# The first expert's rows: a trip through DRAM and VectorE in place of TensorE's transposes, with SyncE's DMAs in a written order

## The chip, the cores and the metric

The kernel is one program on one core of a Trainium2 chip. The core's engines run their own instruction streams, each in its own order, and wait for each other through semaphores: TensorE (PE, matrix products and transposes through a product), VectorE (DVE), ScalarE (ACT), GpSimd (POOL) and SyncE (SP), which here does nothing but issue DMAs. POOL issues the indirect DMAs (gathers and scatters by a list of row numbers). The metric is the device time of one execution in microseconds; the kernel before takes 783.3 us (median of three runs, 783.01 to 784.11).

## The reference

x has 2048 tokens of 448 values. Two branches read it, and a gate mixes them.

```python
# A: linear attention, 16 heads of 28; phi = two softmaxes of a per-head map
phi_q = concat([softmax(pq), softmax(-pq)])         # the same for k
o = (phi_q @ (phi_k^T v)) / (phi_q @ sum(phi_k))
a = o @ wo
# B: 8 experts of 448 -> 1792 -> 448, each token to its best two
logits = x @ w_gate;  topk_idx = argsort(-logits)[:, :2]
for e in range(8):
    out += w[e] * (silu(x @ w1[e]) @ w2[e])         # w is 0 for tokens that did not choose e
g = sigmoid((x * gate_w).sum(-1))
return g * a + (1 - g) * b
```

All of it is float32. The kernel keeps that precision by writing a float32 operand as a rounded high part and a low part, and by adding three products.

## The kernel before, in words

Tokens go in 16 tiles of 128. A first loop makes keys, values, queries and the router's logits, tile by tile. A second loop (`for t in range(NT + 2)`, here called the loop over steps t) finishes the attention: step t does `attend(t)` on PE (product `n`), a chain of small operations on VectorE that ends in `w` (`weigh`), a sum on POOL (`om`), and, one and two steps later, the transposes of `om` on PE (`turn(t - 1)`, product `ot`; rounded to `oh`, `ol`) and the projection (`project(t - 2)`, product `ao`), which ScalarE scales into a buffer `aos` (three of them) that SP stores to the output. `n` of a step has one place in PSUM, so PE starts the next step's `n` when `w` is done with it.

Beside this the experts are prepared. Routing ends some steps into the loop: each token has written its number and weight into a table in DRAM (`tabd`), sorted by expert. The experts are taken by rank of size (`byrank`). `table()` reads each expert's part of `tabd` into `tabm` (512 places, 4 chunks of 128) and, for the three largest experts, `tabx` (places beyond 512, at most 40). `rows(lo, hi)` on POOL turns these tables into row numbers (`idm`, `idx`), and `gather` on POOL fetches the rows of the first expert, in 5 chunks c of 128 tokens (the last of 40), as `xg`. The rows must be turned so that the 448 values lie across partitions (`xgh`, `xgl`, high and low parts): `first_tokens(c)` does it for the first expert, `tokens(e, c)` for the others, later.

The variable `k` counts steps from the one in which the last routing store goes out (k = 1 is t = 7 here, k = 2 is t = 8). At k = 2 the first expert's weights of step 0 are loaded (`load(0)`; a step is 256 of the 1792 columns, two DMAs `wr1` and `wr2`), and `load(1)` stands behind the loop. In the last steps of the loop PE already does the first products of expert 0 (`fill_in`, product `hp`). Then the experts follow, with PE as the busy engine to the end: for each pair of weight steps ScalarE rounds the weights (`w1h`, `w2h`), VectorE subtracts (`w1l`, `w2l`), PE does the first layer (`hp`), ScalarE the silu (`hs`), VectorE splits it (`hx`), PE does the second layer (`acc`).

PE, ACT and DVE run in the order in which the code is written (a manual schedule). POOL's instructions in this part keep the written order too (`in_turn`). SP's DMAs are put in order by a scheduler that estimates times, except where `follow` gives an order: `behind_(i)` makes a DMA stand behind the one that was given to it last (`met["sp"]`). Before, only weight loads were given to it, so the scheduler could place `load(1)` among the loop's stores.

The constants that matter: `ROWS = 1` and `ASKED = {1: (0, 1, 2), 2: (3, 4)}`: chunks 0 to 2 are gathered at k = 2, chunks 3 and 4 at k = 3. `nm = 4` is the number of whole chunks, `P = 128`, `EX = 40`.

Of the kernel before, what the change touches and what calls it, by code (L numbers as in the profile page):

```python
# [8 lines left out]
F32 = mybir.dt.float32  # L9
F32R = mybir.dt.float32r  # L10
BF16 = mybir.dt.bfloat16
I32 = mybir.dt.int32
# [6 lines left out]
P = 128  # L19
# [40 lines left out]
STORES = {}  # L60
LASTS = 1
PLAIN = (2, 3)
VAHEAD = 6
AHEAD = 2
WARM = (4, 3)
# [25 lines left out]
def gated_mix(ctx: ExitStack, tc: tile.TileContext, xt, xq, wk, wq, wv, wphi, wo, w12, out):  # L91
# [15 lines left out]
    def bank(tag, name):  # L107
        pool, n = banks[tag]
        return pool.tile([P, 512], F32, tag=tag, name=name, bufs=n)
# [21 lines left out]
    def in_turn(i, kind=None):  # L131
        if runs["on"]:
            if kind is None or kind != runs["kind"]:
                runs.update(before=runs["last"], last=[], kind=kind)
            for o in runs["before"]:
                follow(i, o)
            runs["last"].append(i)
        return i
# [126 lines left out]
    tabm = cst.tile([P, E * nm, 2], F32, name="tabm")  # L265
    tabx = cst.tile([P, LARGE, 2], F32, name="tabx")
    idm = cst.tile([P, E * nm], I32, name="idm")
    idx = cst.tile([EX, LARGE], I32, name="idx")
    idq = cst.tile([P, E, 4 * nm + 2], I32, name="idq")
    nc.gpsimd.memset(idq, 0)  # L270
    byrank = cst.tile([P, E], I32, name="byrank")
# [505 lines left out]

    raws, wts = {}, {}

    def load(s):  # L780
        e, q = divmod(s, F // 256)
        if q == 0:
            for r in range(e, E if e else 1):
                if r not in whose:
                    whose[r] = nc.values_load(byrank[0:1, r:r + 1], engines=SPONLY, min_val=0, max_val=E - 1)
        keep = narrow(e) and q >= KEPT
        raws[s] = stage(pm, whose[e], q, f"_{s}", 5, (pf, "kept", F // 256 - KEPT) if keep else None)


    def halve(s, layer):  # L790
# [6 lines left out]
        yield  # L797
        nc.vector.tensor_tensor(out=l, in0=raws[s][layer - 1], in1=h.bitcast(F32), op=ALU.subtract)  # L798

    xg = {}  # L800
    x_rows = xq.rearrange("(s a) k -> s (a k)", a=4)

    def extra(e):
# [13 lines left out]
    def gather(e, c, behind):  # L817
        t = pm.tile([P, 4, P], F32, tag="xg", name=f"xg{e}{c}", bufs=nm + 1)
        xg[e, c] = t
        ids, m = (idm[:, e * nm + c:e * nm + c + 1], P) if c < nm else (idx[:, e:e + 1], EX)  # L820
        after(in_turn(nc.gpsimd.indirect_dma_start(out=t[0:m].rearrange("p a k -> p (a k)"), out_offset=None, in_=x_rows,
                                                   in_offset=bass.IndirectOffsetOnAxis(ap=ids, axis=0))), behind)

# [30 lines left out]
        nc.vector.tensor_tensor(out=xl[:, 0:n], in0=src[:, 0:n], in1=xh[:, 0:n].bitcast(F32), op=ALU.subtract)  # L854


    def tokens(e, c):
        if c == 0:
            pool = pf if e % 2 else pw
            xg[e] = (pool.tile([P, 4, CAP], F32R, tag="xgh", name=f"xgh{e}", bufs=1),  # L860
                     pool.tile([P, 4, MAIN] if e >= LARGE else [P, 3, CAP], F32R, tag="xgl", name=f"xgl{e}", bufs=1))
        xgh, xgl = xg[e]
        if (e, c) not in xg:
            return
        t = xg[e, c]
        n, m = (4, P) if c < nm else (-(-extra(e) // 32), extra(e))
        xt_ = pm.tile([P, 4, P], F32, tag="xt", name=f"xgt{e}{c}")
        for b in range(n):
            nc.vector.transpose(xt_[:, :, b * 32:(b + 1) * 32], t[:, b].rearrange("p (c k) -> p c k", c=4))
        yield  # L870
        m = min(m, ROOMS[e] - c * P)
        at = slice(c * P, c * P + m)
        both(xgh[:, :, at], xgl[:, :, at], xt_[:, :, 0:m], e >= LARGE)


    def first_tokens(c):
        m = P if c < nm else EX
        t = xg[0, c][0:m]
        x4 = pm.tile([P, 4, 4, 32], F32, tag="xt", name=f"x40{c}")[0:m]
        in_turn(nc.gpsimd.tensor_copy(x4, t.rearrange("p a (c k) -> p c a k", c=4)))  # L880
        yield
        tp = bank("A", f"xgt0{c}")
        v = tp[:, 0:4 * m].rearrange("p (c n) -> p c n", c=4)
        for i in range(4):
            nc.tensor.transpose(v[:, i], x4[:, i].rearrange("p a k -> p (a k)"), ident[0:m, 0:m])
        if c == 0:
            xg[0] = (pw.tile([P, 4, CAP], F32R, tag="xgh", name="xgh0", bufs=1),
                     pw.tile([P, 3, CAP], F32R, tag="xgl", name="xgl0", bufs=1))
        at = slice(c * P, c * P + m)
        both(xg[0][0][:, :, at], xg[0][1][:, :, at], v)  # L890

    pb_stack.close()
    pc_stack = ExitStack()
# [62 lines left out]
    def leave_row(t, o):  # L958
        ao = pc.tile([P, D], F32, tag="ao", name=f"aos{t}", bufs=3)
        nc.scalar.activation(ao, o[:, 0:D], AF.Copy, scale=gt[:, t:t + 1])  # L960
        rows_done.append(nc.sync.dma_start(out[t * P:(t + 1) * P, :], ao))

    def table():
        for r in range(E):
            v = nc.values_load(byrank[0:1, r:r + 1], engines=SPONLY, min_val=0, max_val=E - 1)
            todo = [(tabm[:, r * nm:(r + 1) * nm], tabd[bass.ds(v * OWN, MAIN), :], P)]
            if r < LARGE:
                n = extra(r)
                for h in range(copies(r)):
                    todo.append((tabx[h * n:(h + 1) * n, r:r + 1], tabd[bass.ds(v * OWN + MAIN, n), :], n))  # L970
            for dst, src, p in todo:
                i = nc.sync.dma_start(dst, src.rearrange("(c p) two -> p c two", p=p))
                after(i, sc)

    def rows(lo, hi):
        in_turn(nc.gpsimd.tensor_scalar(idm[:, lo * nm:hi * nm], tabm.bitcast(I32)[:, lo * nm:hi * nm, 0], float(S - 1), None,
                                op0=ALU.min))
        if lo < LARGE:
            hi = min(hi, LARGE)
            in_turn(nc.gpsimd.tensor_scalar(idx[:, lo:hi], tabx.bitcast(I32)[0:EX, lo:hi, 0], float(S - 1), None, op0=ALU.min))  # L980

    def quarters():
        for a in range(4):
# [267 lines left out]
    for t in range(NT + 2):  # L1251
        if t - 1 in QASKS:
            signs(EQ[QASKS[t - 1]], pq[QASKS[t - 1]])
        elif t == 0:
            signs(EQ[6], pq[6])
        if t < RANKS:
            advance(QSTEPS.get(t, 2))
        early = t in EARLY
        for u in TOPS.get(t, ())[:early]:
            top[u] = tops(EQ[u], f"q{u}", pr)  # L1260
        if at is not None and t == at + 1:
            store(LASTS, behind)
            table()
        if t < NT:
            n_ = attend(t)
        behind = [reached["n"]]
        store(STORES.get(t, 3) if at is None or at == NT else 0, behind)
        if at is None and not routes and t >= RANKS:
            routes.append(ranks())
            at = NT  # L1270
        if at == NT and len(stores) <= LASTS and not routes:
            at = t
        k = t - (NT if at is None else at)
        if k == ROWS + 1:
            rows(0, 1)
        for c in ASKED.get(k - ROWS, ()):
            gather(0, c, behind)
        if t < NT:
            weigh(t, n_)
        advance(2 if t >= RANKS else WSTEPS.get(t, 0))  # L1280
        for u in TOPS.get(t, ())[early:]:
            top[u] = tops(EQ[u], f"q{u}", pr)
        if t + QAHEAD in top:
            drop(EQ[t + QAHEAD], top[t + QAHEAD])
        rows_too = t + 2 < NT
        if rows_too:
            flip(t + 2, True)
            if t >= 1:
                turn(t - 1, True)
        if 1 <= t and t + QAHEAD - 1 < NT:  # L1290
            raise_(t + QAHEAD - 1)
        if t >= 2:
            if t == NT + 1:
                fill_in()
            leave_row(t - 2, project(t - 2))
        if t == NT:
            fill_in()
        if 1 <= t <= NT and not rows_too:
            turn(t - 1, False)
        if t in QASKS:  # L1300
            ask(QASKS[t], some=(0 if t else 5, 11))
        if t == NT - 1:
            fill_in()
        if t == PEND:
            pe_stack.close()
            pm = ctx.enter_context(tc.tile_pool(name="pm", bufs=2, side="right", reuse_waits="tile"))
            pw = ctx.enter_context(tc.tile_pool(name="pw", bufs=1, side="right", reuse_waits="tile"))
            ph = ctx.enter_context(tc.tile_pool(name="ph", bufs=2, side="right", reuse_waits="tile"))
        if k == ROWS + 3:
            rows(1, E)  # L1310
        if k == 2:
            load(0)
            splits += [halve(0, 1), halve(0, 2)]
        part_way()
        if ROWS + 2 <= k < ROWS + 3 + nm:
            g = first_tokens(k - ROWS - 2)
            next(g)
            coming.append(g)
        if SPLIT <= t < SPLIT + 3 and splits:
            if next(splits[0], 0) == 0:  # L1320
                del splits[0]
                if splits:
                    next(splits[0])
# [177 lines left out]
```

## Time and profile before

| | us |
|---|---|
| median of three runs | 783.3 |
| the profiled execution | 784.29 |
| its span, first to last instruction | 782.5 |
| of which: PE busy | 772.5 |
| loop over steps t with the first expert's preparation | about 100 to 210 |
| first `hp` of expert 0 | 201.82 |

The profile is one execution of the program. Its page gives the busy time of each engine, a strip of 40 slices of the span, the DMA queues, and the costliest groups of instructions; the trace behind it can be asked for the instructions of an engine in order of time, for who waited for whom, and for busy times in stretches. A row of a timeline gives start and duration in us, engine, line, operation, what is written and read (`hp<-xgh,w1h`: product hp of xgh and w1h), partitions x elements, how many are merged into the row (x4), and, in brackets, how long the engine sat idle before it and what ended that. `SPq` rows are the issues of DMAs; a DMA's data land later. PE and its weight loads (PEld) overlap.

Two rows of the strip show the whole span, 19.6 us a digit: PE is at nine tenths or more in nearly every slice, and its clock is full in all of them.

```profile
PE   9999999999999999999999999999999999999996
PEclk9999999999999999999999999999999999999999
```

### The profile page before, as it was taken

To read this page: it belongs to the slowest core of one execution; us is meant where nothing else is said; L and a number is where in the kernel's file an instruction comes from. 1 tells how busy PE (TensorE), PEld (TensorE's weight loads), DVE (VectorE), ACT (ScalarE), POOL (GpSimd) and SP (SyncE) were. 2 spreads that over 40 slices of the span, in tenths; PEclk is the share of its full clock that TensorE was granted. 3 is DMA by queue.
4 is the path that set the end of the run, shared out by engine and by line. 5 is a ranking of instruction groups with operands and counts; after the bars stand their busy time and mean duration, and the time that the engine had idled before them with its cause. 6 is when DMAs were issued, how large, how long until landed. Compare 5 with 4: busy or idle time off the path is not lost. (4 is left out here: it accounts for less than half of the span.)

```text
span 782.5 us, 18423 instructions
## 1 busy us (share of the span) xinstructions
PE 772.5 (99%) x7548; PEld 721.0 (92%) x7548; DVE 482.0 (62%) x1047; ACT 308.7 (39%) x521; POOL 338.3 (43%) x320
## 2 busy tenths in 40 slices
PE   9999999999999999999999999999999999999996
PEld 7888888888999999998999799999999999999995
DVE  4798978777775865675566345554744555475442
ACT  5543455666523443343333233333433333343220
POOL 5667877885123226413550237054225405523102
PEclk9999999999999999999999999999999999999999
DMA  8420000044343236324633354364345336434502
GB/s 272 132 87 1 2 2 26 28 101 159 100 164 125 73 113 160 127 93 107 167 114 105 69 142 149 113 156 132 123 119 154 131 115 158 136 129 111 172 3 47
DMA packets 39756, 86.37 MB, mean 110 GB/s; under 512 B 11338, under 2 KB 20722, under 8 KB 39668
## 3 DMA queue, kind: packets, MB, share of 16 engines
q1 hardware_dynamic: 29332, 67.88, 26.1%
q0 software_dynamic: 10192, 17.03, 11.2%
q8 instruction: 61, 1.00, 0.6%
q10 hardware_dynamic: 144, 0.23, 0.1%
q14 instruction: 27, 0.22, 0.1%
HBM read 72.31 MB, written 12.82 MB: 109 GB/s over the span
## 5 line engine op out<-in xcount | busy, mean ns | idle before, releaser
L1127 PE MATMUL acc<-w2h,hx 64*128 64x448 f32 (+3 forms) x1088 | 192.3, 363 | 0.1
L1076 ACT ACTIVATE hs<-hp 128x272 f32<-128x272 f32 (+4 forms) x154 | 70.8, 483 | 305.9 <-issue 192.5
L829 POOL DMA_INDIRECT xg<-in_xq_dram,idq x114 | 126.6, 1111 | 149.5 <-PE hp L1043 52.2
L1082 DVE CAST hx<-hs 128x504 fp32r<-128x504 f32 (+5 forms) x154 | 55.0, 357 | 203.2 <-ACT hs L1076 203.1
L1127 PEld LDWEIGHTS acc<-w2h,hx 64*128 64x128 f32 (+3 forms) x1088 | 160.4, 182 | 4.5 <-ACT y L1216 1.6
L1127 PE MATMUL acc<-w2l,hx 64*128 64x448 f32 (+3 forms) x544 | 154.3, 363 | 0.0
L1043 PE MATMUL hp<-xgh,w1h 64*128 64x504 f32 (+2 forms) x490 | 146.0, 385 | 0.0
L1043 PE MATMUL hp<-xgh,w1l 64*128 64x504 f32 (+2 forms) x490 | 145.9, 385 | 0.0
L1043 PE MATMUL hp<-xgl,w1h 64*128 64x504 f32 (+2 forms) x490 | 145.8, 384 | 0.0
L995 POOL DMA_INDIRECT out_dram<-y,tabm x30 | 49.3, 1643 | 158.1 <-DVE y L1218 150.8
L1161 PE MATMUL acc<-w2h,hx 128*128 128x448 f32 (+2 forms) x362 | 110.6, 365 | 0.0
L1127 PEld LDWEIGHTS acc<-w2l,hx 64*128 64x128 f32 (+3 forms) x544 | 96.4, 182 | 1.2
L1043 PEld LDWEIGHTS hp<-xgh,w1h 64*128 64x128 f32 x490 | 87.4, 184 | 2.2 <-issue 0.3
L1043 PEld LDWEIGHTS hp<-xgl,w1h 64*128 64x128 f32 x490 | 87.5, 185 | 1.8
L1043 PEld LDWEIGHTS hp<-xgh,w1l 64*128 64x128 f32 x490 | 87.5, 185 | 1.7
L1085 DVE TENSOR_TENSOR hx<-hs,hx 128x276 fp32r<-128x276 f32 (+5 forms) x168 | 84.8, 512 | 5.3
L145 PE MATMUL hp<-xgh,w1h 128*128 128x272 f32 (+1 forms) x336 | 87.9, 289 | 0.0
L145 PE MATMUL hp<-xgh,w1l 128*128 128x272 f32 (+1 forms) x336 | 87.8, 289 | 0.0
L798 DVE TENSOR_TENSOR w1l<-wr,w1h 128x1024 fp32r<-128x1024 f32 x56 | 68.2, 1218 | 11.1 <-ACT w1h L796 9.9
L1161 PEld LDWEIGHTS acc<-w2h,hx 128*128 128x128 f32 (+2 forms) x362 | 67.4, 186 | 6.1 <-issue 0.7
L1161 PE MATMUL acc<-w2l,hx 128*128 128x448 f32 (+2 forms) x188 | 68.7, 365 | 0.0
L145 PEld LDWEIGHTS hp<-xgh,w1h 128*128 128x128 f32 x336 | 63.2, 188 | 0.7
(249 smaller groups left out, 1402.8 us busy)
## 6 DMA issues: line engine op xcount, KB each, us to landing
wr<-in_w_dram SPq DMA_DIRECT2D x56, 512.0 KB, 3.6
wr<-in_w_dram SPq DMA_DIRECT2D x46, 448.0 KB, 4.4
kept<-in_w_dram SPq DMA_DIRECT2D x10, 448.0 KB, 4.2
out_dram<-aos SPq DMA_DIRECT2D x16, 224.0 KB, 5.2
xr<-in_xt_dram SPq DMA_DIRECT2D x10, 256.0 KB, 5.0
xg<-in_xq_dram,idq POOLq DMA_INDIRECT x114, 3.4
xr<-in_xt_dram SPq DMA_DIRECT2D x6, 192.0 KB, 4.3
out_dram<-zero SPq DMA_DIRECT2D x5, 224.0 KB, 3.8
```

Of the source, the lines that this page charges most:

```text
L145: reached["pe"] = nc.tensor.matmul(o, a, b, start=i == 0, stop=i == n - 1)
L798: nc.vector.tensor_tensor(out=l, in0=raws[s][layer - 1], in1=h.bitcast(F32), op=ALU.subtract)
L829: i = nc.gpsimd.indirect_dma_start(out=t[:, b], out_offset=None, in_=xq, in_offset=bass.IndirectOffsetOnAxis(ap=idq[:, e, 4 * c + b:4 * c ...
L995: return nc.gpsimd.indirect_dma_start(out=out, out_offset=bass.IndirectOffsetOnAxis(ap=idx_ap, axis=0), in_=y, in_offset=None, compute_op= ...
L1043: meet(("first", i), a, lambda: nc.tensor.matmul(o[i], l, r, start=n == 0, stop=n == len(rounds) - 1), n == 0)
L1076: nc.scalar.activation(hs[:, tsl], hp, AF.Silu)
L1082: nc.vector.tensor_copy(h[:, tsl], hs[:, tsl])
L1085: nc.vector.tensor_tensor(out=h[:, a + o:b + o], in0=hs[:, a:b], in1=h[:, a:b].bitcast(F32), op=ALU.subtract)
L1127: meet((e, c), a, lambda: nc.tensor.matmul(acc[e][c][:l.shape[1], 0:D], l[half[a]], r[half[a]], start=new, stop=ends and c not in of[k + 1 ...
L1161: i = nc.tensor.matmul(acc[e][c][:l.shape[1], 0:D], l, r, start=fc == 0 and k == 0, stop=fc == NFC - 1 and k == len(pr) - 1)
```

## The change

The first expert's rows are no longer turned by PE. POOL's gather is followed by a write of the chunk to DRAM (`rows_out`, `by_row`) and four reads of it back into the same tile (`rows_in`), each of which puts every fourth 128-value quarter of the chunk's rows onto 32 partitions. Then one blockwise transpose on VectorE (`in_blocks`, 32 x 32 blocks) gives the turned rows; the experts that follow use the same function, so that their four transposes a chunk become one instruction. ScalarE rounds the result as before; the two subtractions move from VectorE to POOL (`xsplit(..., nc.gpsimd)`), one step later, and POOL's copies go. The last chunk is gathered with 64 rows, 24 of them row 0, to fill two blocks.

On SP, the loop's stores, the tables and the writes and reads are all given to `behind_`, in the order of the code. `table()` is cut in two: the first expert's table stays at k = 1, the others go to k = 5, and their conversion `rows(1, E)` from k = 4 to k = 7; `load(0)` goes from k = 2 to k = 4.

```diff
+TABLE = 5
+FIRST_LOAD = 4
...
-        for b in range(n):
-            nc.vector.transpose(xt_[:, :, b * 32:(b + 1) * 32], t[:, b].rearrange("p (c k) -> p c k", c=4))
+        in_blocks(xt_, t, n)
...
+    def rows_out(c):
+        m = P if c < nm else 64
+        by_row[c] = dram.tile([m, 4, P], F32, name=f"by_row{c}")
+        behind_(nc.sync.dma_start(by_row[c], xg[0, c][0:m]))
+
+    def rows_in(c):
+        n = 4 if c < nm else 2
+        for a in range(4):
+            behind_(nc.sync.dma_start(xg[0, c][32 * a:32 * a + 32, 0:n],
+                                      by_row[c][:, a].rearrange("(b t) k -> t b k", b=n)))
+
     def first_tokens(c):
-        m = P if c < nm else EX
-        t = xg[0, c][0:m]
-        x4 = pm.tile([P, 4, 4, 32], F32, tag="xt", name=f"x40{c}")[0:m]
-        in_turn(nc.gpsimd.tensor_copy(x4, t.rearrange("p a (c k) -> p c a k", c=4)))
-        yield
-        tp = bank("A", f"xgt0{c}")
-        v = tp[:, 0:4 * m].rearrange("p (c n) -> p c n", c=4)
-        for i in range(4):
-            nc.tensor.transpose(v[:, i], x4[:, i].rearrange("p a k -> p (a k)"), ident[0:m, 0:m])
+        n, m = (4, P) if c < nm else (2, EX)
+        xt_ = pm.tile([P, 4, P], F32, tag="xt", name=f"xgt0{c}")
+        in_blocks(xt_, xg[0, c], n)
+        yield
...
-        both(xg[0][0][:, :, at], xg[0][1][:, :, at], v)
+        xsplit(xg[0][0][:, :, at], xg[0][1][:, :, at], xt_[:, :, 0:m], nc.gpsimd)
...
         rows_done.append(nc.sync.dma_start(out[t * P:(t + 1) * P, :], ao))
+        behind_(rows_done[-1])
...
-            table()
+            table(0, 1)
...
-        if k == ROWS + 3:
+        if k == TABLE:
+            table(1, E)
+        if k == TABLE + 2:
             rows(1, E)
-        if k == 2:
+        if k == FIRST_LOAD:
             load(0)
...
-        if ROWS + 2 <= k < ROWS + 3 + nm:
-            g = first_tokens(k - ROWS - 2)
+        for lag, move in ((1, rows_in), (0, rows_out)):
+            for c in ASKED.get(k - ROWS - lag, ()):
+                move(c)
+        if ROWS + 3 <= k < ROWS + 4 + nm:
+            g = first_tokens(k - ROWS - 3)
```

What this makes of the engines' order is seen in the built programs. First SP in the second half of the loop. The rows are its DMAs, destination and source; `aos5` is the buffer of step 5's store, `xg00` chunk 0 of the first expert, `wr1_0` and `wr2_0` the weights of step 0. Before, from the last table load on:

```order
L972 DMA tabm_143<-tabd_155 128x4x2
L961 DMA out_0_dram<-aos5_2632 128x448
...
L773 DMA wr1_0_2779<-in_w12_dram 128x1024
...
L773 DMA wr2_0_2780<-in_w12_dram 128x896
...
L773 DMA wr1_1_3573<-in_w12_dram 128x1024
...
L773 DMA wr2_1_3574<-in_w12_dram 128x896
L961 DMA out_0_dram<-aos6_2754 128x448
L961 DMA out_0_dram<-aos7_2884 128x448
```

And of the change, from store 7 to the first of the 15 tables of the other experts:

```order
L972 DMA out_0_dram<-aos7_2792 128x448
L891 DMA xg00_2602<-by_row0_2685 32x4x128 x4
L891 DMA xg01_2604<-by_row1_2687 32x4x128 x4
L891 DMA xg02_2606<-by_row2_2689 32x4x128 x4
L886 DMA by_row3_2807<-xg03_2726 128x512
L886 DMA by_row4_2809<-xg04_2728 64x512
L972 DMA out_0_dram<-aos8_2906 128x448
...
L776 DMA wr1_0_2909<-in_w12_dram 128x1024
...
L776 DMA wr2_0_2910<-in_w12_dram 128x896
L891 DMA xg03_2726<-by_row3_2807 32x4x128 x4
L891 DMA xg04_2728<-by_row4_2809 32x2x128 x4
L972 DMA out_0_dram<-aos9_3016 128x448
...
L984 DMA tabm_143<-tabd_156 128x4x2
```

Twenty reads, two of the five writes and the first weights now stand between store 7 and the tables, which stood ahead of store 5. The second weight step (`wr1_1`, `wr2_1`), which followed the first, stands at the end of the loop, behind store 15:

```order
L972 DMA out_0_dram<-aos14_3495 128x448
L972 DMA out_0_dram<-aos15_3553 128x448
...
L776 DMA wr1_1_3569<-in_w12_dram 128x1024
...
L776 DMA wr2_1_3570<-in_w12_dram 128x896
...
L776 DMA wr1_2_3573<-in_w12_dram 128x1024
```

Here `wr1_1` moved from behind `wr2_0` to behind `aos15`, and `wr1_2` with it. Second, POOL in steps 11 to 14; `om11` is the sum of step 11, `idm` of 28 columns and `idx` are the conversion of the other experts' tables. Before:

```order
L976 TENSOR_SCALAR idm_145<-tabm_143 128x28
L980 TENSOR_SCALAR idx_146<-tabx_144 40x2
L880 COPY x401_2999<-xg01_2688 128x512
L931 TENSOR_TENSOR om11_3043<-w11_3041 128x448
...
L880 COPY x402_3105<-xg02_2690 128x512
L931 TENSOR_TENSOR om12_3149<-w12_3147 128x448
```

And of the change:

```order
L942 TENSOR_TENSOR om13_3253<-w13_3251 128x448
L989 TENSOR_SCALAR idm_145<-tabm_143 128x28
L993 TENSOR_SCALAR idx_146<-tabx_144 40x2
L160 TENSOR_TENSOR xgh0_3104<-xgt02_3209,xgh0_3104 64x128
L161 TENSOR_TENSOR xgl0_3105<-xgt02_3209,xgh0_3104 128x3x128
L942 TENSOR_TENSOR om14_3357<-w14_3355 128x448
```

The conversion moved from ahead of `om11` to behind `om13`, and the copies of the chunks gave way to two subtractions each, those of chunk 2 between the conversion and `om14`.

More of the change, by code (lines that the diff above doesn't have):

```diff
@@ L267, in gated_mix @@
     idm = cst.tile([P, E * nm], I32, name="idm")
-    idx = cst.tile([EX, LARGE], I32, name="idx")
+    idx = cst.tile([64, LARGE], I32, name="idx")
+    nc.gpsimd.memset(idx, 0)
     idq = cst.tile([P, E, 4 * nm + 2], I32, name="idq")
@@ L778, in gated_mix, with expert @@
     raws, wts = {}, {}
+    def expert(r):
+        if r not in whose:
+            whose[r] = nc.values_load(byrank[0:1, r:r + 1], engines=SPONLY, min_val=0, max_val=E - 1)
+        return whose[r]
     def load(s):
         e, q = divmod(s, F // 256)
[L782 to L785, printed above, removed]
         keep = narrow(e) and q >= KEPT
-        raws[s] = stage(pm, whose[e], q, f"_{s}", 5, (pf, "kept", F // 256 - KEPT) if keep else None)
+        raws[s] = stage(pm, expert(e), q, f"_{s}", 5, (pf, "kept", F // 256 - KEPT) if keep else None)
     def halve(s, layer):
@@ L798, in halve @@
         nc.vector.tensor_tensor(out=l, in0=raws[s][layer - 1], in1=h.bitcast(F32), op=ALU.subtract)
-    xg = {}
+    xg, by_row = {}, {}
     x_rows = xq.rearrange("(s a) k -> s (a k)", a=4)
@@ L819, in gather @@
         xg[e, c] = t
-        ids, m = (idm[:, e * nm + c:e * nm + c + 1], P) if c < nm else (idx[:, e:e + 1], EX)
+        ids, m = (idm[:, e * nm + c:e * nm + c + 1], P) if c < nm else (idx[:, e:e + 1], 64)
         after(in_turn(nc.gpsimd.indirect_dma_start(out=t[0:m].rearrange("p a k -> p (a k)"), out_offset=None, in_=x_rows,
@@ L854, in both, with in_blocks @@
         nc.vector.tensor_tensor(out=xl[:, 0:n], in0=src[:, 0:n], in1=xh[:, 0:n].bitcast(F32), op=ALU.subtract)
+    def in_blocks(out_, t, n):
+        nc.vector.transpose(out_[:, :, 0:n * 32].rearrange("p c (b k) -> p b c k", b=n),
+                            t[:, 0:n].rearrange("p b (c k) -> p b c k", c=4))
     def tokens(e, c):
@@ L961, in leave_row, with table @@
         rows_done.append(nc.sync.dma_start(out[t * P:(t + 1) * P, :], ao))
-    def table():
-        for r in range(E):
-            v = nc.values_load(byrank[0:1, r:r + 1], engines=SPONLY, min_val=0, max_val=E - 1)
+        behind_(rows_done[-1])
+    def table(lo, hi):
+        for r in range(lo, hi):
+            v = expert(r)
             todo = [(tabm[:, r * nm:(r + 1) * nm], tabd[bass.ds(v * OWN, MAIN), :], P)]
@@ L973, in table @@
                 after(i, sc)
+                behind_(i)
     def rows(lo, hi):
@@ L979, in rows @@
             hi = min(hi, LARGE)
-            in_turn(nc.gpsimd.tensor_scalar(idx[:, lo:hi], tabx.bitcast(I32)[0:EX, lo:hi, 0], float(S - 1), None, op0=ALU.min))
+            in_turn(nc.gpsimd.tensor_scalar(idx[0:EX, lo:hi], tabx.bitcast(I32)[0:EX, lo:hi, 0], float(S - 1), None, op0=ALU.min))
     def quarters():
```

## The prediction

> **What bounds the kernel now.** I read the page's first part, then the list of what TensorE (PE) waited for over the whole span, then the timelines of each engine between 155 and 216 us, the only stretch in which the first expert's rows are prepared.
>
> ```profile
> PE 772.5 (99%) x7548; PEld 721.0 (92%) x7548; DVE 482.0 (62%) x1047; ACT 308.7 (39%) x521; POOL 338.3 (43%) x320
> ...
> PE n L910 <- DVE w L926: 1.4, 2, 1.0
> ```
>
> PE is busy for 772.5 of 782.5 us, and the longest of its waits for another engine's line is 1.4 us in two pieces (the list gives the sum, the count and the longest). So the time moves by what PE no longer executes, and by each new wait of PE, one for one: the experts that follow have no slack in which PE could catch up. I call a step of the loop over token tiles t; `n`, `om`, `ot`, `ao` of step t are its attention, its sum on GpSimd (POOL), its transpose and its output projection.
>
> **What goes from PE.** First the five transposes of the expert's rows, then the two stalls that stand among them.
>
> ```profile
> 177.14 0.60 PE L885 MATMUL xgt<-ident,x 128*128 128x128 f32 x4
> 177.67 1.16 PE L910 MATMUL n<-B,et 64*64 64x60 f32 x64
> ...
> 184.80 0.47 PE L145 MATMUL ao<-WHo,oh 128*128 128x448 f32 x1 [0.23 <-ACT aos L960]
> ...
> 188.72 1.29 PE L910 MATMUL n<-B,et 64*64 64x60 f32 x64 [0.97 <-DVE w L926]
> ...
> 197.66 0.44 PE L885 MATMUL xgt<-ident,x 40*128 40x40 f32 x4
> 198.03 1.16 PE L910 MATMUL n<-B,et 64*64 64x60 f32 x64
> ...
> 201.47 0.60 PE L943 MATMUL ot<-ident,om 128*128 128x128 f32 x4
> ```
>
> A group of four holds PE from 177.14 to 177.67, 0.53 us; four such groups and the small one (197.66 to 198.03, 0.37) make **2.49 us**. The stalls of 0.23 and 0.97, **1.20 us**, come from one store:
>
> ```profile
> 184.11 0.63 ACT L960 ACTIVATE aos<-ao,gt 128x448 f32<-128x448 f32 x1 [2.14 <-DMA out_dram<-aos]
> ```
>
> ScalarE waited 2.14 us for a buffer of `aos`, whose store stood behind four weight loads. Stores 5 to 8 now go ahead of all weights, so this goes. Next in line is VectorE, whose `w` the `n` of the next step waits for. It gives up two subtractions a step and gets one transpose; the trace has four small ones of the same total size:
>
> ```profile
> 178.49 0.29 DVE L853 TENSOR_TENSOR xgh<-xgt,xgh 64x128 fp32r<-64x128 f32 x1
> 178.80 0.56 DVE L854 TENSOR_TENSOR xgl<-xgt,xgh 128x384 fp32r<-128x384 f32 x1
> ...
> 180.63 1.09 DVE L926 TENSOR_TENSOR w<-n,r 128x896 f32<-128x896 f32 x1
> ...
> 182.52 1.16 PE L910 MATMUL n<-B,et 64*64 64x60 f32 x64
> ...
> 253.82 0.88 DVE L869 STREAM_TRANSPOSE xgt<-xg 128x128 f32<-128x128 f32 x4
> 254.62 1.05 DVE L798 TENSOR_TENSOR w2l<-wr,w2h 128x896 fp32r<-128x896 f32 x1
> ```
>
> That is 0.80 us (253.82 to 254.62) against 0.85 given up, so `w` ends as it did, 0.80 ahead of `n` (181.72 against 182.52), and 0.53 less on PE leaves 0.27: nothing is added or won. The same edit in the later experts lies beside a PE that never waits for it: nothing. Alone, these parts would bring `ot` of step 14 from 201.47 to 201.47 - 3.69 = **197.78**.
>
> **What the tables cost.** The other experts' 15 table loads leave their place before the weights and stand behind 20 read-backs of the rows. On POOL the conversion that needs all 15 (`rows(1, E)`) now stands between `om` of 13 and of 14, with two subtractions of chunk 2 behind it; all are ahead of `om` of 14, and `ot` of 14 needs that. Before, the conversion ran at 179.57 without a wait. So I follow SyncE (SP), from the last point that the change leaves alone: store 7 waits for `aos` of 7, whose activation starts at 172.92 and lasts 0.63.
>
> ```profile
> 172.92 0.63 ACT L960 ACTIVATE aos<-ao,gt 128x448 f32<-128x448 f32 x1 [0.27 <-PE ao L145]
> ...
> 175.62 22.75 SPq L961 DMA_DIRECT2D out_dram<-aos  x7
> ...
> 176.09 22.27 SPq L961 DMA_DIRECT2D out_dram<-aos  x6
> ...
> wr<-in_w_dram SPq DMA_DIRECT2D x1, 512.0 KB, 3.6
> wr<-in_w_dram SPq DMA_DIRECT2D x1, 448.0 KB, 5.5
> ...
> 162.01 0.41 SPq L972 DMA_DIRECT2D tabm<-tabd  x1
> ...
> 169.03 3.48 SPq L972 DMA_DIRECT2D tabm<-tabd  x4
> 169.61 2.90 SPq L972 DMA_DIRECT2D tabm<-tabd  x3
> ...
> 172.13 0.37 SPq L972 DMA_DIRECT2D tabm<-tabd  x1
> ...
> DMA to landing us min/median/max: 2.0/3.3/3.8
> ```
>
> Plain issues stand 0.47 apart (175.62 to 176.09). From 173.57, 16 of them (store 7, twelve read-backs, two writes, store 8) end at 181.1. The two loads of weight step 0 follow at 181.1 and 181.7. In the built program SP's DMAs share eight completion counters in turn, so each waits until the one eight before it has landed; the last read-back so waits for the second weight load, 181.7 + 5.5 = 187.2. With store 9 the tables start near **187.8** (186.8 with a landing halfway between the two rows, 189 if each issue ahead takes 0.07 more). Fifteen tables took 162.01 to 172.13 before, 0.72 a step among gathers; undisturbed a step is 0.58 (169.03 to 169.61). I take 0.64 for 14 steps, 9.0 us, and a landing of 2.5 between the last row's 2.0 and 3.8: **199.3**, with ends 186.8 + 8.1 + 2.0 = 196.9 and 189 + 10.1 + 3.8 = 202.9. POOL's share behind that:
>
> ```profile
> 179.57 0.29 POOL L976 TENSOR_SCALAR idm<-tabm 128x28 int32<-128x28 int32 x1
> 179.93 0.21 POOL L980 TENSOR_SCALAR idx<-tabx 40x2 int32<-40x2 int32 x1
> ...
> 63.12 0.46 POOL L158 TENSOR_TENSOR XH<-xr,XH 64x128 fp32r<-64x128 f32 x1
> 63.65 1.01 POOL L159 TENSOR_TENSOR XL<-xr,XH 128x384 fp32r<-128x384 f32 x1
> ...
> 197.97 1.14 POOL L931 TENSOR_TENSOR om<-w 128x448 f32<-128x448 f32 x1 [3.33 <-DVE w L926]
> ```
>
> The conversion takes 0.36 to its second part and 0.21 for that; then 0.53 and 1.01 for the subtractions (rows of the key stage, same shapes) and 1.14 for `om`; with 0.15 of handing over 3.4 us. So `ot` of 14 runs at 199.3 + 3.4 = **202.7**, and PE idles 4.9 us there. VectorE is held too: its transpose of chunk 4 takes the buffer of chunk 2, so it waits for the same subtraction, and `w1l` of the first weights, the attention chain of 15 and `oh`, `ol` of 14 stand behind it.
>
> ```profile
> 199.86 1.22 DVE L798 TENSOR_TENSOR w1l<-wr,w1h 128x1024 fp32r<-128x1024 f32 x1
> ...
> 203.87 0.56 DVE L159 TENSOR_TENSOR ol<-ot,oh 128x384 fp32r<-128x384 f32 x1
> ...
> 204.93 0.78 PE L145 MATMUL ao<-WHo,ol 128*128 128x448 f32 x3
> ```
>
> From `w1l` to the end of `ol` were 4.57 us (199.86 to 204.43). Now the subtraction ends at 201.5, the transpose at 201.9, so `ol` at 206.5; `ao` of 14 wants it 3.46 after `ot` (201.47 to 204.93), at 206.15. With 0.1 for the first `hp`, which waits for `w1l`, that is **0.45** more. Against before PE is then 202.7 - 201.47 + 0.45 = 1.7 us late. This wait also covers the rest: if read-backs landed late and VectorE held PE earlier, up to 4.9 us of it would cost nothing, as would POOL's ten added subtractions. If the tables came early, that cover would be gone.
>
> **What the second weight step costs.** `load(1)` was half of the four loads at 173.31 to 175.5; now it stands behind store 15, which waits for the very last `aos`.
>
> ```profile
> 211.21 0.64 ACT L960 ACTIVATE aos<-ao,gt 128x448 f32<-128x448 f32 x1 [1.84 <-PE ao L145]
> 211.74 1.05 ACT L796 ACTIVATE w1h<-wr 128x1024 fp32r<-128x1024 f32 x1
> ...
> 215.26 0.29 PE L145 MATMUL hp<-xgh,w1h 128*128 128x276 f32 x1
> ...
> 173.31 2.21 SPq L773 DMA_DIRECT2D wr<-in_w_dram  x4
> ```
>
> In the times of before: `aos` of 15 ends at 211.85, its store goes, the load follows 0.6 later (the pitch of the tables) at 212.45, landing between the 3.6 and 5.5 of the two rows above; I take 3.9, near the first, with the store just ahead of it: 216.4. Then `w1h` on ScalarE, 1.05, and `w1l` on VectorE, 1.22: 218.7. PE has work until its `hp` at 215.26 and needs `w1l` from the second matmul on: it waits **3.45 us** (a little less than 218.7 - 215.26 + the hand-overs, since its first matmul needs only `w1h`). The `silu` of the piece before stands behind `w2h` on ScalarE, so the next second layer waits 0.3 more. Nothing hides this; before, the cover was that the load went out 37 us earlier. By the landings it is 3.1 (3.6, and no later wait) to 5.3 in all; I take 3.75.
>
> **The sum.** -2.49 - 1.20 + 4.92 + 0.45 + 3.75 = **+5.4 us**. The profiled execution took 784.29 (span 782.5 and 1.8 around it), so 789.7 for one like it; its median of three is 783.3, 1.0 lower, so 788.7.
>
> **The rivals.**
>
> *The tables land in time* (not slower). The point is 197.78 - 3.4 = 194.4 for the last table. Then PE keeps its 3.69 us and pays only for `load(1)`, 3.1 to 3.75: -0.6 to +0.1, 782.7 to 783.4. For it: POOL and VectorE have room. Against: the low end of the tables is 196.9.
>
> *The queue is slower*: read-backs and tables at the slow ends, 202.9, give 3.6 more, and a `load(1)` at its slow end 1.6: 792.3 to 793.9. For it speaks the 0.72 a step; against, that the gathers which disturbed it are over.
>
> *The clock falls in the long wait.* In this trace it is 1.00 for four microseconds after PE's last matmul, which ends at 775.99, and lower after that:
>
> ```profile
> 778.00:780.00 2.00, 0.00 (x0) 1.00 0.35 97
> 780.00:782.50 2.50, 0.00 (x0) 0.57 0.03 10
> ```
>
> My first wait is 4.9 us, the second 3.5, so the first may reach that point. If PE then ran at 0.57 for as long as it took to fall, 4 us, it would lose 4 x 0.43 = 1.7: 790.4. [...]
>
> *Faster*: both waits are covered by something that I don't see, leaving -3.69: 779.6. Only a load that lands at once would do it, against every landing row above.
>
> **How the numbers follow.** Forecast 62%, slower queue 12%, fallen clock 14%, tables in time 9%, both covered 3%. The range goes from the tables' low end with the cheapest `load(1)` (-3.69 + 2.52 + 0.45 + 3.1 = +2.4, lowered a little towards the rival in time) to the slow queue: 785.0 to 792.5, leaving out the 12% below and a part of the slow queue. A measurement of this kernel tells 0.2%, 1.6 us, from no change; slower by more than that 88%, within it 9%, faster 3%.
>
> **What would show it.** No `xgt` matmuls on PE; PE waiting at `ot` of 14 for `om`, POOL at `idm` (28 columns) for a table; SP's last table issued near 197, `wr` of step 1 after the last store, and PE waiting over 3 us at the third pair of `hp`. If POOL doesn't wait at `idm`, or PE has less than 2 us of waits beside the old ones, the forecast is wrong.

## The result: 794.3 us, slower, and past the end of the range

The changed kernel takes 794.33 us (median of 5 runs, 792.99 to 795.65) against 783.30 before: a ratio of 1.0136, 95% interval 1.0126 to 1.0147. The forecast was 788.7 in a range of 785.0 to 792.5. The direction was right, and the loss is twice the predicted one: 11.0 us instead of 5.4. The profiled execution took 794.56; its span is 792.8, 10.3 longer than before.

First the same lines of the page as before: PE's busy time, and the two strips.

```profile
PE 774.1 (98%) x7528; PEld 721.2 (91%) x7528; DVE 478.4 (60%) x958; ACT 309.1 (39%) x521; POOL 340.9 (43%) x326
...
PE   9999999999689999999999999999999999999997
...
PEclk9999999999899999999999999999999999999999
```

PE has 20 instructions fewer (7528 against 7548) and is nevertheless busy 1.6 us longer. Two slices, the 11th and 12th (198 to 238 us), are no longer full, and in the 11th the clock isn't either. Then the list of what PE waited for, by line: sum, count, longest.

```profile
PE ot L954 <- POOL om L942: 6.3, 1, 6.3
PE hp L147 <- ACT w1h L800: 2.0, 1, 2.0
...
PE hp L147 <- DVE w1l L802: 0.9, 1, 0.9
```

Both predicted waits are there, at the predicted instructions: `ot` of step 14 for `om` 14, and the first `hp` of weight step 1 for its weights. PE's timeline, with the rows that stand against 201.47, 215.26 and the matmul of before with the same place in the program:

```profile
206.02 1.11 PE L954 MATMUL ot<-ident,om 128*128 128x128 f32 x4 [6.31 <-POOL om L942]
...
214.79 0.37 PE L147 MATMUL ao<-WHo,oh 128*128 128x448 f32 x1
...
223.44 0.40 PE L147 MATMUL hp<-xgh,w1h 128*128 128x276 f32 x1 [2.00 <-ACT w1h L800]
224.70 0.39 PE L147 MATMUL hp<-xgh,w1l 128*128 128x276 f32 x1 [0.86 <-DVE w1l L802]
...
231.85 0.29 PE L147 MATMUL hp<-xgh,w1h 128*128 128x276 f32 x1
```

The same points of before's timeline:

```profile
208.77 0.36 PE L145 MATMUL ao<-WHo,oh 128*128 128x448 f32 x1
...
220.89 0.29 PE L145 MATMUL hp<-xgh,w1h 128*128 128x276 f32 x1
```

So PE is 4.55 us late at `ot` 14 (206.02 against 201.47), 6.02 at `ao` 15 (214.79 against 208.77), 8.18 at the first `hp` of weight step 1 and 10.96 at that of step 2 (231.85 against 220.89). That is the whole loss (the spans differ by 10.3), and no wait of PE follows. The prediction had 1.23 (202.7), 1.68, and, with the 3.75 of `load(1)`, 5.43 at the last. Its missing 5.5 us lie in three places: 3.3 before `ot` 14, 1.0 between `ot` 14 and `ao` 15, and 1.2 behind that.

Why `ot` 14 is late is read on SP and POOL. A row's second number is the time from the first issue of a run to the end of its last.

```profile
174.03 0.34 SPq L972 DMA_DIRECT2D out_dram<-aos  x1
174.47 7.06 SPq L891 DMA_DIRECT2D xg<-by_row  x12
181.63 1.00 SPq L886 DMA_DIRECT2D by_row<-xg  x2
...
183.53 0.90 SPq L776 DMA_DIRECT2D wr<-in_w_dram  x2
184.52 6.15 SPq L891 DMA_DIRECT2D xg<-by_row  x8
...
191.93 0.41 SPq L984 DMA_DIRECT2D tabm<-tabd  x1
...
200.99 17.23 SPq L972 DMA_DIRECT2D out_dram<-aos  x6
```

```profile
202.68 0.30 POOL L989 TENSOR_SCALAR idm<-tabm 128x28 int32<-128x28 int32 x1 [10.63 <-DMA tabm<-tabd]
...
204.83 1.13 POOL L942 TENSOR_TENSOR om<-w 128x448 f32<-128x448 f32 x1
```

The order is the predicted one, POOL waits at `idm` for a table, and from `idm` to `ot` it takes 3.34 us (predicted 3.4). But the tables start at 191.93 instead of 187.8. The largest part of that is in the twelve read-backs, which hold SP for 7.16 us (174.47 to 181.63) where 0.47 apart would be 5.64. Taken one by one, eleven of them stand 0.42 to 0.53 apart; the third alone lasts 1.80:

```profile
175.47 1.80 SPq L891 DMA_DIRECT2D xg<-by_row  x1
```

The clock is the other part. Windows of 1 us; the columns behind the width are busy times of PE, PEld, DVE, ACT and POOL with their counts, then the granted clock, the DMA share and GB/s.

```profile
202.00:203.00 1.00, 0.00 (x0) 0.00 (x0) 0.00 (x0) 0.00 (x0) 0.30 (x1) 0.57 0.82 301
203.00:204.00 1.00, 0.00 (x0) 0.00 (x0) 0.00 (x0) 0.63 (x1) 0.78 (x3) 0.50 0.98 369
208.00:209.00 1.00, 1.00 (x6) 1.00 (x6) 0.93 (x3) 1.00 (x1) 0.45 (x1) 0.52 0.06 16
209.00:210.00 1.00, 1.00 (x8) 0.96 (x7) 0.94 (x3) 0.63 (x3) 0.43 (x1) 1.00 0.00 0
...
224.00:225.00 1.00, 0.30 (x2) 0.30 (x3) 0.97 (x4) 0.69 (x2) 0.00 (x0) 1.00 0.95 387
225.00:226.00 1.00, 1.00 (x10) 1.00 (x9) 0.93 (x5) 0.53 (x1) 0.00 (x0) 1.00 0.67 158
226.00:227.00 1.00, 1.00 (x6) 1.00 (x6) 1.00 (x2) 0.82 (x2) 0.00 (x0) 0.52 0.77 188
...
229.00:230.00 1.00, 1.00 (x5) 0.92 (x4) 1.00 (x2) 1.00 (x2) 0.00 (x0) 0.78 0.04 8
```

It falls to half in the first wait (0.57 is 0.14 at full speed and the rest at half, so at 202.14, 2.4 us after PE's last work) and returns at 208.96, three microseconds after PE is at work again. It falls a second time near 226.04, when the second wait is already over, and returns at 229.44.

### The profile page after: what moved, and what is told of

Its sections match the earlier page's. It is cut to its first block, busy times and chain, and to the rows that moved or that the text cites. A ratio compares the mean times of both kernels' runs of the same rounds, so it can differ in the third digit from the quotient of the medians.

```text
span 792.8 us, 18372 instructions
## 1 busy us (share of the span) xinstructions
PE 774.1 (98%) x7528; PEld 721.2 (91%) x7528; DVE 478.4 (60%) x958; ACT 309.1 (39%) x521; POOL 340.9 (43%) x326
## 5 line engine op out<-in xcount | busy, mean ns | idle before, releaser
L147 PE MATMUL hp<-xgh,w1h 128*128 128x272 f32 (+1 forms) x336 | 89.5, 293 | 2.0 <-ACT w1h L800 2.0
L147 PE MATMUL hp<-xgh,w1l 128*128 128x272 f32 (+1 forms) x336 | 89.4, 293 | 0.9 <-DVE w1l L802 0.9
```

What stands on the lines that cost most here:

```text
L147: reached["pe"] = nc.tensor.matmul(o, a, b, start=i == 0, stop=i == n - 1)
```

## The experiments

All ratios are to the kernel before, run on the same chip in the same session: 783.91 us for the first four kernels, 783.37 for the last four, so that times of different sessions compare to about 0.6 us. The first question was whether the two waits are separate and worth what they seem to be.

**Load of weight step 1 earlier.** In the changed kernel:

```diff
         if k == TABLE:
             table(1, E)
+            load(1)
...
-    load(1)
     held = []
```

> The change, with load(1) issued right behind the other experts' tables (step 11) in place of behind store 15. Theory A (two waits made by order, each followed by a fall of the clock): PE's wait at the third pair of hp (3.3 us against before) and the half clock behind it (1.65 us) both go, the wait at ot of 14 stays: 794.3 - 4.9 = 789.4 (788.5 to 790.5). Rival B (the trip through DRAM and its traffic cost the time, the late weights only share it): no more than the shown wait of 2.9 us goes, 791 or above.

Measured: 789.65 us (789.50 to 790.75), ratio 1.0079 (1.0063 to 1.0096), as theory A has it. PE's list has the wait at `ot` (7.4 us) and none at `hp`; the mean clock is 0.995, against 0.991. So `load(1)` behind the loop and what follows from it cost about 4.7 us (794.33 to 789.65, across two sessions; in the traces, from `ot` 14 to the `hp` of weight step 2, it is 4.5), more than the 3.75 of the prediction, which has no clock in it.

**The conversion moved out of the way of `om` 14.**

```diff
-        if k == TABLE + 2:
-            rows(1, E)
...
+    rows(1, E)
     assert not coming and not splits
```

> The change, with the conversion of the other experts' tables, rows(1, E), behind the last subtraction of the first expert's rows on POOL in place of between om of 13 and 14. Theory A: the tables land as late as before (202 to 203) but nobody waits; ot of 14 runs at about 199.6 in place of 206.0, and the clock does not fall there (1.0 to 1.5 us): 794.3 - 6.5 - 1.5 = 786.4 (785.4 to 787.8). Rival B: ot of 14 then waits for something else that the trip made late (read-backs, POOL's subtractions), and the time stays above 789.

Measured: 791.40 us (791.30 to 792.04), ratio 1.0097 (1.0080 to 1.0114): a miss for theory A, and in the range of rival B, though not at B's place. The wait at `ot` 14 is gone, but another stands behind it, at `ao` 14. The rows are of PE, ACT and SP of this kernel:

```profile
204.37 0.47 PE L147 MATMUL ao<-WHo,oh 128*128 128x448 f32 x1 [3.68 <-ACT oh L159]
```

```profile
203.20 0.63 ACT L971 ACTIVATE aos<-ao,gt 128x448 f32<-128x448 f32 x1 [5.72 <-DMA out_dram<-aos]
```

```profile
197.94 2.70 SPq L984 DMA_DIRECT2D tabm<-tabd  x5
200.74 14.21 SPq L972 DMA_DIRECT2D out_dram<-aos  x6
```

`aos` has three buffers. The activation of row tile 13 needs the buffer of store 10, and store 10 stands behind the 15 tables (200.74, the first of the six). On ScalarE `oh` of 14 stands behind that activation, and PE's `ao` of 14 needs `oh`. The same wait is in the changed kernel, under the longer one for `om`:

```profile
203.24 0.63 ACT L971 ACTIVATE aos<-ao,gt 128x448 f32<-128x448 f32 x1 [4.92 <-DMA out_dram<-aos]
```

It ends at 203.24, before `om` 14 is ready, and so costs nothing there.

**Both edits.**

> The two edits together (load(1) behind the tables, rows(1, E) behind the last subtraction). Theory A: both waits and both falls go, 794.3 - 7.9 - 4.9 = 781.5 (780.5 to 783), which is before less the transposes (2.5) and the store's stall (1.2) plus some 2 us for VectorE's wait for read-backs and the like; clock 1.0 until PE ends. Rival B: 784 or above, slower than before, with waits left in the steps 10 to 15.

Measured: 791.99 us (791.02 to 792.22), ratio 1.0101 (1.0085 to 1.0118): a second miss for theory A. Its expectation was written before the third wait was known. No `om` and no `hp` wait is left, and the third has grown to 8.9 us. The two weight loads (201.10) now stand ahead of store 10 as well: it goes out 1.5 us later than in the run before this one, and its buffer comes free 5.6 us behind its issue (207.84 on ScalarE) instead of 2.5.

```profile
209.01 0.74 PE L147 MATMUL ao<-WHo,oh 128*128 128x448 f32 x1 [8.86 <-ACT oh L159]
```

```profile
202.22 18.29 SPq L972 DMA_DIRECT2D out_dram<-aos  x6
```

**Only the stores' order, in the kernel before.** This tests the price of `load(1)` without any of the rest.

```diff
         rows_done.append(nc.sync.dma_start(out[t * P:(t + 1) * P, :], ao))
+        behind_(rows_done[-1])
```

> The kernel before with one line of the change: the loop's stores are given to behind_, so that load(1) goes behind store 15; the transposes on PE and the tables stay as they were. Theory A: PE waits about 3.3 us at the third pair of hp and then loses 1.65 us to the clock if a window falls so; the stall of 1.2 us goes since only two weight loads stand ahead of store 7: 783.3 + 3.3 + 1.65 - 1.2 = 787.0 (785 to 788.5). Rival B (late weights cost little without the trip's traffic): within 1.6 us of 783.3.

Measured: 788.07 us (786.08 to 789.34), ratio 1.0061 (1.0044 to 1.0077). One added line in the kernel before gives the same two waits at `hp`, to a hundredth:

```profile
215.78 0.39 PE L145 MATMUL hp<-xgh,w1h 128*128 128x276 f32 x1 [1.99 <-ACT w1h L796]
217.03 0.39 PE L145 MATMUL hp<-xgh,w1l 128*128 128x276 f32 x1 [0.86 <-DVE w1l L798]
...
222.87 0.29 PE L145 MATMUL hp<-xgh,w1h 128*128 128x276 f32 x1
```

The four runs differ more than most, and with the clock: 786.08, 787.70, 788.44 and 789.34 us at mean granted clocks of 0.999, 0.997, 0.997 and 0.994. Only the run of 786.08 has a trace, and in it the clock stays full; from the other means, the same wait brings a fall in some executions and none in others. Without one it cost 3.4 us, since this edit also takes the 1.2 of the store stall away (783.91 - 1.20 = 782.71). In the traces, from the first `hp` to that of weight step 2, it is 3.61 (200.19 to 222.87, before 201.82 to 220.89).

Then the question was whether three waits, with the clock, are all. A table load that stands behind store 12 instead of store 9 has no store behind it whose buffer is wanted again (16 row tiles, three buffers), and its conversion comes behind `om` 15.

**Tables three steps later, and `load(1)` ahead of them.**

```diff
-TABLE = 5
+TABLE = 8
...
+        if k == 5:
+            load(1)
...
-    load(1)
     held = []
```

> The change with the 15 tables issued three steps later (behind store 12 instead of store 9, so that no store whose buffer is needed again stands behind them; their conversion on POOL moves with them, behind om of 15) and load(1) two steps ahead of them. Theory A (three waits hide each other: om 14 behind the tables' conversion, the store buffers behind the tables, hp behind load(1), and nothing else stands behind them): all three go, PE has no wait over 1 us between 195 and 235 us, the clock stays full, and the time is before's 783.9 on this chip less the 3.7 us of PE's transposes and store stall, plus 0.5 lost early: 780.7 (779.9 to 782.0), faster than before. Theory B (a fourth consumer is behind): a new wait of PE of 2 us or more, 782.5 or more.

Measured: 781.03 us (780.18 to 781.68, 8 runs), ratio 0.9971 (0.9960 to 0.9981): faster than both kernels. No wait of PE between 195 and 235 us is left, and the clock stays full. PE's timeline at the places of the result:

```profile
198.41 0.60 PE L954 MATMUL ot<-ident,om 128*128 128x128 f32 x4
...
212.21 0.29 PE L147 MATMUL hp<-xgh,w1h 128*128 128x276 f32 x1
```

`ot` 14 is 3.06 us ahead of before (198.41 against 201.47) and the `hp` of weight step 1 is 3.05 ahead. That is what the removed transposes and the removed store stall are worth, with what else the change does up to there. POOL still waits 4.9 us for the tables, but nothing stands behind it:

```profile
207.72 0.30 POOL L989 TENSOR_SCALAR idm<-tabm 128x28 int32<-128x28 int32 x1 [4.89 <-DMA tabm<-tabd]
```

**Tables three steps later, alone** (`TABLE = 8` and nothing else).

> The change with the 15 tables three steps later and nothing else: load(1) stays behind the loop. Theory A (the waits add up, and load(1)'s price is that of the run of before with its stores in order, 3.3 us and up to 1.7 for a fallen clock): PE waits only at hp for w1h and w1l of step 1, 2.9 us in two pieces, none at ot 14 or at ao 14: 780.7 + 3.3 = 784.0 to 785.7. Theory B (the tables, now just ahead of the last stores, delay load(1) too): the wait at hp is over 4 us and the time 786 or more.

Measured: 786.04 us (785.07 to 787.01), ratio 1.0031 (1.0019 to 1.0043). The waits are theory A's, 2.1 and 0.9 at `hp` and none at `ot` or `ao` 14; the time is 0.3 above its upper end and so at the foot of theory B's range, whose wait of over 4 us did not come. Behind the same two waits that brought no fall of the clock in the trace of the stores' order, there is one in the profiled run here (0.50 from 218 to 220 us, mean 0.995; over the six runs 0.993 to 0.999). So the tables' place is worth 8.3 us (794.33 to 786.04), and `load(1)` 5.0 more (786.04 to 781.03), near the 4.7 that it was with the tables in their first place.

**Products of zeros in the waits.** This leaves every wait as it is and keeps PE at work.

```diff
             tp = bank("O", f"ot{t}").rearrange("p (c n) -> p c n", n=P)
+            if t == 14:
+                for _ in range(6):
+                    nc.tensor.matmul(tp, blank[:, 0], blank.to_broadcast([P, 4, P]), start=True, stop=True)
...
         hp = bank("A", f"hp{e}_{fc}_{hf}")[:, 0:n]
+        if (e, fc, hf) == (0, 2, 0):
+            for _ in range(4):
+                nc.tensor.matmul(hp[:, 0:2 * P].rearrange("p (r c) -> p r c", r=2), blank[:, 0],
+                                 blank.to_broadcast([P, 2, P]), start=True, stop=True)
```

> The change with products of zeros on PE inside its two waits, into PSUM banks whose real products come right behind and overwrite them: six of 128x512 ahead of the four ot of step 14, four of 128x256 ahead of the first hp of step 1's weights. No wait is taken away: POOL's om 14 and the weights come when they come. Theory A (the rest of the loss, beside the waits, is the clock): the granted clock stays at 1.00 to the end, ot of 14 to ao of 15 takes 7.3 to 7.8 us instead of 8.8, the hp pieces after the second wait take 0.29 us a matmul instead of 0.43, and the time falls by 2 to 3 us to 791.3 to 792.3. Theory B (those stretches are long because VectorE and ScalarE come late, or the products of zeros push the real ones back): 793.8 or more.

Measured: 792.10 us (791.85 to 795.20), ratio 1.0120 (1.0103 to 1.0137). The median is 2.2 lower than that of the changed kernel, as theory A has it, but the intervals of the two ratios overlap, so the reading rests on the trace. PE's timeline:

```profile
199.05 5.31 PE L955 MATMUL ot<-blank 128*128 128x512 f32 x12
...
205.31 0.66 PE L957 MATMUL ot<-ident,om 128*128 128x128 f32 x4 [0.94 <-POOL om L942]
...
206.39 0.40 PE L147 MATMUL hp<-xgh,w1l 128*128 128x276 f32 x1 [0.30 <-DVE w1l L802]
...
213.60 0.37 PE L147 MATMUL ao<-WHo,oh 128*128 128x448 f32 x1
...
222.26 0.40 PE L147 MATMUL hp<-xgh,w1h 128*128 128x276 f32 x1 [0.28 <-ACT w1h L800]
...
229.35 0.29 PE L147 MATMUL hp<-xgh,w1h 128*128 128x276 f32 x1
```

The clock is 1.00 in every window from 196 to 236 us. From `ot` 14 to `ao` 15 are 8.29 us, against 8.77 in the changed kernel and 7.30 before: the clock was 0.48 of the excess 1.47. The other 0.99 is there at full clock too and is VectorE's: the second `hp`, which wants `w1l`, runs 1.08 behind `ot` instead of 0.56, and `ao` 14 then stops for VectorE's part of `oh` and for `ol`. That is a miss against my 7.3 to 7.8. From the first `hp` of weight step 1 to that of step 2 are 7.09 us against 8.41: the clock was 1.32. The run with only the stores' order, without products of zeros and with a full clock, has the same 7.09 (215.78 to 222.87), so the zeros themselves add nothing there. The two falls cost 1.8 us, with the waits left in place. That the time also fell by about 2 is in part luck: in this trace `ot` 14 is 0.71 early already (205.31 against 206.02), where the edit takes nothing away.

**All tables first** (left at k = 1 with the first expert's; `load(1)` at k = 5).

```diff
-            table(0, 1)
+            table(0, E)
...
         if k == TABLE:
-            table(1, E)
+            load(1)
...
-    load(1)
     held = []
```

> The change with all tables left at k = 1, where they were before, and load(1) issued at k = 5 (behind the read-backs). The conversion has its tables in time and no store stands behind them, but the first writes of rows wait for 15 issues, about 4.5 us. Theory A (only the place of the tables costs; rows 4.5 us later cost VectorE's transpose of chunk 0, 179.4 us, a wait of 2 to 3 us, of which PE feels what is over 0.8): no wait of PE at ot 14, ao 14 or hp, one of 1 to 2.5 us near 182 at n: 781.5 to 783.5. Theory B (rows late hold VectorE in several steps): waits of PE over 3 us between 180 and 200, 784 or more.

Measured: 784.37 us (782.80 to 787.37, 11 runs), ratio 1.0014 (1.0002 to 1.0026). The time is 0.9 above theory A's range and in theory B's. The mechanism is A's: between 150 and 240 us PE has a single wait, the 2.5 that ends at 184.15, at the upper end of what A had:

```profile
PE n L921 <- DVE w L937: 3.0, 2, 2.5
```

The rows come back later, VectorE's first transpose waits 2.66 us for them, and `n` waits for VectorE. The clock falls behind it once more, with PE fully busy, which A did not count. A window of this kernel:

```profile
186.00:187.00 1.00, 1.00 (x13) 0.88 (x12) 0.81 (x4) 0.70 (x2) 0.98 (x1) 0.50 0.66 213
```

So in this order the tables do have to move for the rows to come in time; the change only moved them to a place where others wait for them.

## Why the prediction was wrong, by its own steps

*What goes from PE* (-3.69): right in kind, somewhat too large. Where nothing else is in the way it is 3.05 us in the trace. Of the missing 0.64, the execution was 0.10 late before any of it (the `n` ahead of the first transposes at 172.91 against 172.81), and a new wait of `n` for `w` is 0.19, where I had left 0.27 of slack; the rest stays open. Both are read in the run with the tables later and `load(1)` earlier (the wait ends at 182.00). In the time it is 2.3 (781.03 against 783.37); the profiled execution of before was itself 0.9 us above the median of that session.

*What the tables cost*: the mechanism was right and its size wrong. The failing step is the sum on SP, which has 16 issues end at 181.1 and the tables start at 187.8. Its pitch, "Plain issues stand 0.47 apart", also holds for the read-backs, whose rows no trace of before has: in the run with all tables first the twelve take 5.64 us, which is 0.47 each.

```profile
176.72 5.64 SPq L891 DMA_DIRECT2D xg<-by_row  x12
```

What the sum left no room for is a single issue that lasts longer, as the third of the twelve did here. The 4.1 us from 187.8 to 191.93 are:

- 0.46 by which store 7 was already late in this execution (174.03 against 173.57);
- 1.5 in the twelve read-backs, nearly all of it that one issue;
- 0.5 in the two writes and store 8 (1.90 us against 1.41);
- 0.8 because the last read-back went out 6.3 us behind the second weight load (184.09 to 190.37) instead of 5.5;
- 1.0 from there to the first table (1.56 against 0.6), where the issue of store 9 alone lasts 0.96; 0.1 was gained elsewhere.

The tables, quicker than assumed, give 0.75 back. The bound "189 if each issue ahead takes 0.07 more" was drawn too near: the 16 issues took 0.12 more on the average. The trace of before had such an issue too, a table load of 1.77 us at 170.18; I took it into the mean of "0.72 a step among gathers" and put it down to the gathers.

*VectorE held* (+0.45): right in kind, 0.99 measured (in the run with products of zeros). `w1l`, which lasts 1.77 us beside `om` on POOL where I had taken 1.22, would account for all of the difference:

```profile
205.28 1.77 DVE L802 TENSOR_TENSOR w1l<-wr,w1h 128x1024 fp32r<-128x1024 f32 x1
```

*The second weight step* (+3.75): right, in size too. From `ao` 15 to the `hp` of weight step 2 PE lost 10.96 - 6.02 = 4.94 us, and without the clock's 1.32 that is 3.62; the run with only the stores' order, at full clock, has 3.61. The parts fit as well: the second matmul, which wants `w1l`, comes 3.29 late against `ao` 15 (224.70 against 215.39, less 6.02), where I had 3.45. The sign that I gave, over 3 us of waiting at the third pair of `hp`, was just missed in the list (2.0 and 0.9), which leaves out the matmul between the two. In the time the step was worth 4.7 to 5.0, clock included.

*The clock*: this is the other step that failed, as a judgement. The sum puts it at nothing, and it stood as a rival with 14%, for one fall, costing 1.7 us. It came twice, for 1.8 us. The 0.57 by which I priced it is the mean of a window that holds both speeds; in the windows above the low one is 0.50. I went by one row of before, in which the clock stays full for 4.4 us behind PE's last matmul (775.99 to 780.35), so that only the longer of my two waits could reach a fall. The distance was not the same here: the first fall of the change came 2.4 us after PE's last work, and the second 1.3 us after its second wait had ended (224.70 to 226.04). Nor did the clock return with the work: the first fall lasts 6.82 us (202.14 to 208.96), 2.9 of them with PE at work again, and the second 3.40, with PE at work all through (226.04 to 229.44). The mean clock is 0.991 to 0.994 in the five runs of the change, against 0.999 in the profiled run of before. With 14% I had it far too low.

*What was not in it*: the third wait, for the buffer of store 10 behind the tables. It cost nothing in the changed kernel, but it decided the two repairs that I tried first: taking away only the longest wait that the profile shows gave 2.9 of some 8 us.

*The rivals*: neither "tables in time" nor "covered by something" came. Of "the slower queue" (tables 3.6 us later, 792.3 to 793.9) the tables' part came, 3.3 us, and `load(1)` at its slow end did not; "the clock falls" (790.4) came with it. The forecast's 5.4, with 3.3 for SP, 0.5 for VectorE, 1.8 for the clock and 0.1 off `load(1)`, makes the 10.96. I had given each rival its chance as if the other stayed away, and the range ended at 792.5.

The prediction's reading that an issue waits until the one eight before it has landed fits the trace. Of the 6.15 us of the last eight read-backs (184.52 to 190.67) the list of what SP waited for gives 1.9 to the landing of the two weight loads; the first of the eight lasts 1.19, and the others stand about 0.47 apart:

```profile
SPq L891 <- DMA wr<-in_w_dram: 1.9, 2, 1.8
```

What stays open is why now and then an issue lasts more than 1.1 us. In each of the eight traces that have read-backs one or two of the twenty do (1.15 to 1.93 us).

## What to carry to other kernels

Putting DMAs of one queue into a written order also puts each one behind all that is written ahead of it: for every load or store that is moved, list who wants its data or its buffer next, and when, since several such waits can hide under the longest (here 6.3 us over a second one, that showed itself only when the first was gone). A run of many issues is to be priced by what such a run took in all, with room for a few long ones, and not by the usual pitch alone: here one issue of 1.80 us made most of what twelve took too long. And a wait on TensorE of two or three microseconds is to be priced with the slow clock that may follow (here 1.3 us behind waits of 2.0 and 0.9), which is paid by work that no longer waits.

## What the runs showed of the hardware

Three falls of the clock came after different amounts of idle time. In the changed kernel the first came 2.4 us after PE's last work (199.72 to 202.14), and PE had been busy for 0.97 of the 3.40 us before it (a stretch as long as the second fall). The second met work that had begun again: of the 3.40 us before it (222.64 to 226.04) PE was busy for about 1.7 (0.40 at 223.44, 0.30 in 224 to 225, all from 225 on). In before, PE did nothing in the 3.40 us ahead of the fall at 780.35. Nor did the waits alone decide whether a fall came. The run with only the stores' order has the two waits of the changed kernel (1.99 and 0.86 us against 2.00 and 0.86, with one product between them), and its products behind them take 0.29 us each, as at full clock; in the changed kernel, from 226.10 on, they take 0.43. What decides it was not shown.

Some operations of VectorE and of POOL took longer beside one of the other engine: `w1l` 1.77 us beside `om`, instead of 1.22 (shown above), and POOL's subtraction of a chunk 2.03 beside `w1l`, where it takes 1.01 otherwise (the run with the tables later and `load(1)` earlier):

```profile
192.78 1.01 POOL L161 TENSOR_TENSOR xgl<-xgt,xgh 128x384 fp32r<-128x384 f32 x1
...
197.03 2.03 POOL L161 TENSOR_TENSOR xgl<-xgt,xgh 128x384 fp32r<-128x384 f32 x1
```

In both places the instruction that began first kept its usual time (`om` 1.13, `w1l` 1.18 from 197.01), and the other one got longer.
